# Two own sums moved ahead of other work in a kernel's head, with a rounding, two scalings and one diagonal

## The chip, the cores and the metric

The kernel runs on one core of one Trainium2 chip. The metric is the device time of one execution in microseconds (us), the median over the runs. The engines are TensorE (PE), VectorE (DVE), ScalarE (ACT), GpSimd (POOL) and SyncE (SP, which here only issues DMAs). Each engine works through its own queue in program order.

## The reference

Two stages. The first is a linear attention with a decaying state, for 4 batches, 8 heads, 768 steps and head size 48:

```python
for t in range(S):
    kt, vt, rt = (k[:, :, t], v[:, :, t], r[:, :, t])
    cur = np.einsum('bhd,bhe->bhde', u[None] * kt, vt)
    y[:, :, t] = np.einsum('bhd,bhde->bhe', rt, state + cur)
    state = w[None, :, :, None] * state + np.einsum('bhd,bhe->bhde', kt, vt)
```

Its output, as 3072 tokens of 384 numbers, goes through a gated feed-forward block with 1536 hidden numbers:

```python
g = x @ w_gate
silu = g * (1.0 / (1.0 + np.exp(-g)))
val = x @ w_val
return silu * val @ w_out
```

The three weight matrices arrive as 64-bit floats and are rounded to 32 bits on the chip.

## The kernel before, in words

The attention is cut into 24 units. Unit `i` is 128 steps of one batch: `divmod(i, 4)` gives the piece of the sequence and the batch. For one unit the kernel does this:

- `load(i)`, `load_v(i)`: SP issues the DMAs of k, r and v.
- `own_begin(i)`, `own_end(i)` (together `own_product`, L254 and L257): POOL multiplies r by k, then by u. `own_sum(i)` (L265): DVE sums over the head size. The result `du` is each step's product with itself, one number for each head.
- `diagonal(i)` writes `du` on the diagonal of `At[i % 2]`, the 128x128 score matrices of 8 heads. Units below 4 have four heads done by ACT (L364, one activation for each head) and four by POOL (L371, one instruction).
- `turn(i)`: PE transposes k and r (L385); for units below 4 DVE multiplies the results by tables of powers of w (L387).
- `scores(i)`: PE multiplies keys and rows (L454); then DVE copies the part above the diagonal into `At`, under a mask, in two instructions (L464). These are called the masks of unit i below. They need the diagonal to be in place.
- `outputs(i)`: PE multiplies `At` by v (L507), and ACT copies the result to xT (L511).
- `update(i)`: PE multiplies scaled keys by v (L522); DVE, and for later pieces POOL, bring the states Z up to date (L532 to L535). `scale_k(i)` and `scale_r(i)` (L341, L344) scale k and r on POOL by tables in SBUF. The four `scale_k` of the head work in place in the tile `hats`.

The weights come in 18 chunks of 768 KB. For each, `load_weights` issues the DMA (L179), into one of three buffers. Rounding a chunk takes ACT (`round_high` for each half, L199, through one of two PSUM banks; `round_low`, L205), DVE (`round_dve` for each half, L214 and L215) and POOL (`add_low` for a half, L223, or `round_pool` for a whole chunk, L242). `round_act` is all of ACT's and DVE's part of one chunk, and the issue of a later chunk's DMA.

`gate_value(g, f)` is one group of the feed-forward block: 12 matmuls on PE (L545), a Silu on ACT (L551) and a product on DVE (L552). `queue` puts the groups into a list, and `feed` takes the next one whose weight chunks have been rounded.

The order of the first four units, called the head, is written out by hand from L1204 on: the instructions of each engine are queued in the order of these calls. From L1281 on a loop goes over the units, one `turn`, one `scores`, one `outputs` in each pass, with roundings and `feed` calls in the gaps. After the attention the rest of the feed-forward block follows.

These lines of the head are the ones in which the predicted steps lie, up to the loop:

```python
own_sum(0); own_begin(1); diagonal(0); own_end(1); flush()
...
scores(0); own_sum(1); diagonal(1); flush()
...
feed(1); own_sum(2); diagonal(2); flush(); own_product(3); turn(3)
scores(2); update(0); update(1); scale_k(4); own_sum(3)
feed(1); diagonal(3); flush(); scores(3); scale_k(2); outputs(2)
round_act(); scale_k(3); outputs(3); scale_r(4); round_act()
```

(`flush` queues the ACT activations of a diagonal. The calls stand one to a line in the code.)

Of the kernel before, what the change touches and what calls it, by code (L numbers as in the profile page):

```python
# [22 lines left out]
def fast(  # L23
# [28 lines left out]
    HP = H // 2  # L52
# [65 lines left out]
    def raw(i):  # L118

        if i < 4:  # L120
            return khat[i][:, :, 0:D], rhat[i % 2][:, :, 0:D]
        return k_ld[i % 2][:], r_ld[i % 2][:]
# [46 lines left out]
    def next_chunk(stage):  # L169
        n = done[stage]  # L170
        done[stage] = min(n + 1, NW)
        return n if n < NW else None

    def load_weights():
        n = next_chunk("load")
        if n is not None:
            src = chunks[n][0].bitcast(INT32)
            bits[n] = three.tile([P, WN, 2], INT32, name="w_bits", tag="w_bits")
            sp.dma_start(  # L179
                out=bits[n][:].rearrange("p (c f) two -> p c (f two)", c=src.shape[1]), in_=src  # L180
            )
# [13 lines left out]
    def round_high(n, half, bank):  # L195
        hi = halves(bits[n][:, :, 1], n)[half]
        mag = banks[2 + bank][:, 0 : WN // 2].bitcast(INT32)
        mags[n, half] = mag.rearrange("p (c f) -> p c f", c=hi.shape[1])
        act.activation(  # L199
            mags[n, half].bitcast(FP32), hi.bitcast(FP32), AF.Copy, scale=float(2.0**-112)  # L200
        )

    def round_low(n):
        lows[n] = two.tile([P, WN], INT32, name="w_low", tag="w_low")
        act.activation(  # L205
            lows[n][:], bits[n][:, :, 0].bitcast(UINT32), AF.Copy, scale=float(2.0**-29)
        )

    def round_dve(n, half):
        hi = mags.pop((n, half))  # L210
        f = hi.shape[2]
        dst = chunks[n][1].bitcast(INT32)
        dst = dst[:, :, half * f : half * f + f] if hi.shape[1] == 3 else dst[:, half : half + 1]
        dve.tensor_scalar(dst, hi, -(1 << 31), None, ALU.bitwise_and)  # L214
        dve.scalar_tensor_tensor(dst, hi, 3, dst, ALU.logical_shift_left, ALU.bitwise_or)  # L215
# [6 lines left out]
        low = lows[n][:].rearrange("p (c f) -> p c f", c=dst.shape[1])  # L222
        pool.tensor_tensor(dst[:, :, cols], dst[:, :, cols], low[:, :, cols], ALU.add)  # L223

    def round_act(next_load=1):
        n = next_chunk("act")
        if n is not None:
            round_high(n, 0, 0)
            round_low(n)
            round_dve(n, 0)  # L230
            round_high(n, 1, 1)
            round_dve(n, 1)
            del bits[n]
            for _ in range(next_load):
                load_weights()

    def round_pool():
        n = next_chunk("pool")
# [12 lines left out]
    def own_begin(i):  # L251
        kl, rl = raw(i)
        rks[i] = two.tile([P, H, D], FP32, name="rk", tag="rk")[:]
        pool.tensor_mul(rks[i], rl, kl)  # L254

    def own_end(i):
        pool.tensor_mul(rks[i], rks[i], ub)  # L257

    def own_product(i):
        own_begin(i)  # L260
        own_end(i)

    def own_sum(i):
        dus[i] = three.tile([P, H], FP32, name="du", tag="du")
        dve.tensor_reduce(dus[i][:], rks.pop(i), axis=AX.X, op=ALU.add)  # L265
# [71 lines left out]

        return HP - 1 - a if i >= BLOCKS and i % 2 == (i < SWAPPED) else a

    def scale_k(i):  # L340
        pool.tensor_mul(khat[i % 4][:, :, 0:D], raw(i)[0], kscale)  # L341

    def scale_r(i):
        pool.tensor_mul(rhat_of(i)[:, :, 0:D], raw(i)[1], rscale)  # L344
# [6 lines left out]
    def keep_natural_tables():  # L351
        for bank, dst in zip(banks, (kscale, rscale)):
            act.copy(dst, bank[:].rearrange("p (h x) -> p h x", h=H)[:, :, 0:D])
# [2 lines left out]
        scale_k(i)  # L356
        scale_r(i)

    def diagonal(i):

        du = dus.pop(i)
        on_act = HP if i < 4 else H
        small.extend(
            lambda h=h: act.activation(  # L364
                At[i % 2][:, h, :], ident[:], AF.Identity, scale=du[:, h : h + 1]
            )
            for h in range(on_act)
        )
        if on_act < H:
            n = H - on_act  # L370
            pool.tensor_mul(  # L371
                At[i % 2][:, on_act:H], ident[:].unsqueeze(1).to_broadcast([P, n, P]),
                du[:, on_act:H].unsqueeze(2).to_broadcast([P, n, P]),
            )
# [4 lines left out]
    def turn(i):  # L379
        kr = khat[i % 4], rhat_of(i)  # L380
        tps = [next_psum(HP, P) for _ in kr]
        turned[i] = three.tile([P, HP, P], FP32, name="rT", tag="rT")
        for tp, t, dst, table in zip(tps, kr, (kT[i % 2], turned[i]), (pw[:, :, 1 : P + 1], pv)):
            for a in range(HP):
                pe.transpose(tp[:, a, :], pair(t, a), ident[:])  # L385
            if i < 4:
                dve.tensor_mul(dst[:], tp[:], table)  # L387
            else:
                act.copy(dst[:], tp[:])
# [48 lines left out]
    def scores(i):  # L438

        while lazy:  # L440
            lazy.popleft()()
        ps = [next_psum(HP, P) for _ in range(2)]
        whole, left, right = slice(0, P), slice(0, 64), slice(64, P)
        if i < SWAPPED:
            parts = [(a, whole, whole) for a in range(HP)]
        else:
            parts = []
            for a in range(HP // 2):
                parts += [(a, left, whole), (a, right, right)]
                parts += [(a + HP // 2, right, whole), (a + HP // 2, left, left)]  # L450
        for a, keys, cols in parts:
            for e in range(2):
                rows = slice(64 * e, 64 * e + D)
                pe.matmul(  # L454
                    ps[e][keys, a, cols],
                    kT[i % 2][rows, at(i, a), keys], turned[i][rows, at(i, a), cols],
                    start=True, stop=True, skip_group_check=True,
                )

        def masked_copy(e):  # L460
            if i < SWAPPED:
                dst = At[i % 2][:].rearrange("p (a e) t -> p a e t", e=2)[:, :, e]
                m = mask[:, 0].bitcast(INT32).unsqueeze(1).to_broadcast([P, HP, P])
                dve.copy_predicated(dst, m, ps[e][:])  # L464
                return
            dst = At[i % 2][:].rearrange("p (o a e) t -> p o a e t", o=2, e=2)[:, :, :, e]
            m = mask[:].bitcast(INT32).unsqueeze(2).to_broadcast([P, 2, HP // 2, P])
            dve.copy_predicated(dst, m, ps[e][:].rearrange("p (o a) t -> p o a t", o=2))

        for e in range(2):  # L470
            lazy.append(lambda e=e: masked_copy(e))
        lazy.popleft()()
        if i < BLOCKS:
            lazy.popleft()()
# [38 lines left out]
    def update(i):  # L513
        c, b = divmod(i, B)
        if c == NCH - 1:
            return
        kh, vl, z = khat[i % 4], v_ld[i % 4], Z[b]
        ps = next_psum(HP, D)
        for a in range(HP):
            for q in range(4):  # L520
                e, half = divmod(q, 2)
                pe.matmul(  # L522
                    ps[32 * q : 32 * q + 32, a, :], kh[:, 2 * a + e, 32 * half : 32 * half + 32],
                    vl[:, a, 64 * e : 64 * e + D],
                    start=True, stop=True, skip_group_check=True,
                )
        for e in range(2):
            rows = slice(64 * e, 64 * e + D)
            ze = z[rows, :, D * e : D * e + D]
            w = w128[rows].unsqueeze(2).to_broadcast([D, HP, D])  # L530
            if c == 0:
                dve.tensor_mul(ze, ps[rows], w)  # L532
            else:
                dve.tensor_add(ze, ps[rows], ze)  # L534
                pool.tensor_mul(ze, ze, w)  # L535
# [663 lines left out]
    def flush():  # L1199
        while small:  # L1200
            small.popleft()()
# [4 lines left out]
    dve.tensor_copy(w128[:].unsqueeze(2), pw[:, :, 0:1])  # L1206
    own_sum(0)
    own_begin(1)
    diagonal(0)
    own_end(1)  # L1210
    flush()
    load(2)
    turn(1)
    keep_natural_tables()
    round_high(0, 0, 0)
    round_low(0)
    load(3)
# [1 line left out]
    load_v(2)  # L1219
    load_v(3)  # L1220
    scores(0)
    own_sum(1)
    diagonal(1)
    flush()
    round_dve(0, 0)
    add_low(0, 0)
    scores(1)
    outputs(0)
    round_high(1, 0, 1)
    round_low(1)  # L1230
    round_dve(1, 0)
    add_low(1, 0)
    own_product(2)
    outputs(1)
    turn(2)
    scale_k(0)
    scale_k(1)
    queue(0)
    for n in range(2):
        round_high(n, 1, n)  # L1240
# [6 lines left out]
    load(5)  # L1247
    feed(1)
    own_sum(2)
    diagonal(2)  # L1250
    flush()
    own_product(3)
    turn(3)
    scores(2)
    update(0)
    update(1)
    scale_k(4)
    own_sum(3)
    feed(1)
    diagonal(3)  # L1260
    flush()
    scores(3)
    scale_k(2)
    outputs(2)
    round_act()
    scale_k(3)
    outputs(3)
    scale_r(4)
    round_act()
    own_product(4)  # L1270
    round_pool()
    update(2)
    update(3)
    load_v(4)
    feed(1)
    round_pool()
# [503 lines left out]
```

## Time and profile before

| | |
|---|---|
| median of 4 runs | 592.11 us (591.30 to 592.57) |
| the profiled execution's own time | 592.64 us |
| its span, first to last instruction | 590.9 us |
| granted TensorE clock | 0.998 |
| busy: PE, DVE, ACT, POOL | 579.6, 421.8, 225.5, 355.2 us |
| HBM read, written | 28.31 MB, 4.72 MB |

The profile is that of one execution. A row of its timeline reads: start in us, duration in us, engine, line, operation, output tile and input tiles, shapes, count, and in brackets the idle time of the engine before it with what ended it. Several equal instructions in a row are one row. A row of the waits reads: who waited, for what, us in total, times, the longest. A row of the table by stage gives the stretch, its length, and for PE, PE's weight loads, DVE, ACT and POOL the busy us and the instructions, then the granted clock, the DMA engines' busy share and GB/s. The time between the start of one instruction and that of the next on an engine is often a little shorter than the duration, since they overlap.

### The profile page before, as it was taken

What the parts mean: (1) busy time and instruction counts of PE and PEld (TensorE: products, weight loads), DVE (VectorE), ACT (ScalarE), POOL (GpSimd) and SP (SyncE); (2) the same over time, 40 slices, a digit from 0 to 9 for tenths busy, and PEclk for the clock granted to TensorE, in tenths of its full rate; (3) what the DMA queues carried; (4) which work ended last, traced back from release to release, by engine and by line L of the source; (5) the groups of instructions that cost most, each with busy time, mean ns of one, the idle gap of its engine ahead of it and who ended that gap; (6) DMA issues with size and microseconds to landing.
All of it is one profiled execution on the core that took longest, in us unless ns stands there. A gap on an engine that the chain in (4) does not pass through costs nothing.

```text
span 590.9 us, 13188 instructions
## 1 busy us (share of the span) xinstructions
PE 579.6 (98%) x5210; PEld 520.6 (88%) x5210; DVE 421.8 (71%) x703; ACT 225.5 (38%) x517; POOL 355.2 (60%) x378
## 2 busy tenths in 40 slices
PE   8889999999999999999999999999999999999996
PEld 7778888899888899988899988889988899888896
DVE  6887786489588777577887477779257878377672
ACT  3479786221343422245332345423134320233410
POOL 5899888989999403877601996412678960011610
PEclk9999999999999999999999999999999999999999
DMA  8999979442342323133234233300100000100001
GB/s 199 225 230 248 282 237 90 67 67 50 75 78 33 56 44 73 47 62 55 40 54 92 58 60 49 48 11 2 54 2 0 2 1 1 55 0 1 1 1 57
DMA packets 148292, 41.48 MB, mean 70 GB/s; under 512 B 138497, under 2 KB 142082, under 8 KB 148226
## 3 DMA queue, kind: packets, MB, share of 16 engines
q1 hardware_dynamic: 144914, 36.27, 30.0%
q10 hardware_dynamic: 3312, 4.33, 2.0%
q8 instruction: 42, 0.69, 0.5%
q14 instruction: 24, 0.20, 0.1%
HBM read 28.31 MB, written 4.72 MB: 56 GB/s over the span
## 4 chain that ended last, share of the span: by engine, by line
PE 91%; POOL 3%; DVE 2%; SPq 2%; issue 1%; DMA 0%; ACT 0%; POOLq 0%; DVEq 0%
PE bank L801 28%; PE bank L620 18%; PE ring L801 13%; PE bank L545 10%; PE bank L1027 9%; PE ring L507 6%; PE ring L454 3%; SPq L411 2%; PE ring L385 1%; POOL s L731 1%; PE ring L522 1%; PE ring L296 1%; POOL At L371 1%; DVE At L464 1%; DVE hv L825 0%
## 5 line engine op out<-in xcount | busy, mean ns | idle before, releaser
L825 DVE TENSOR_TENSOR hv<-hv,bank 128x512 f32<-128x512 f32 x132 | 87.2, 681 | 26.2 <-PE bank L801 15.2
L545 PE MATMUL bank<-xT,wgv 128*128 128x256 f32 x288 | 66.2, 384 | 0.0
L364 ACT ACTIVATE At<-ident,du 128x128 f32<-128x128 f32 x176 | 59.9, 398 | 16.6 <-DVE du L265 7.9
L801 PE MATMUL bank<-xf,wgv 128*128 128x256 f32 x256 | 65.9, 382 | 0.0
L825 ACT COPY hv<-bank 128x512 f32<-128x512 f32 x72 | 40.1, 585 | 57.5 <-PE bank L801 51.2
L545 PEld LDWEIGHTS bank<-xT,wgv 128*128 128x128 f32 x288 | 53.4, 190 | 7.9
L731 POOL TENSOR_TENSOR s<-wgv 128x256 f32<-128x256 f32 x39 | 29.8, 787 | 49.0 <-PE bank L620 48.9
L801 PEld LDWEIGHTS bank<-xf,wgv 128*128 128x128 f32 x256 | 47.8, 190 | 7.0 <-DVE kT L1072 0.6
L1081 POOL TENSOR_TENSOR hv<-At,hats 128x512 f32<-128x512 f32 x8 | 10.2, 1273 | 66.3 <-ACT At L1080 66.3
L535 POOL TENSOR_TENSOR Z<-Z,w 48x192 f32<-48x192 f32 x32 | 16.9, 528 | 36.8 <-DVE Z L534 35.6
L507 PE MATMUL ring<-At,v_ld 128*32 128x128 f32 x768 | 35.6, 273 | 3.4 <-DVE At L464 3.2
L832 ACT ACTIVATE hv<-hv 128x512 f32<-128x512 f32 (+1 forms) x33 | 21.2, 668 | 45.3 <-DVE hv L825 45.2
L801 PE MATMUL bank<-xT,wgv 128*128 128x256 f32 x144 | 35.8, 381 | 0.0
L801 PE MATMUL bank<-xT,s 128*128 128x256 f32 x152 | 35.5, 381 | 0.2 <-POOL s L731 0.2
L507 PEld LDWEIGHTS ring<-At,v_ld 128*32 128x32 f32 x768 | 30.5, 110 | 5.0 <-DVE At L464 4.9
L620 PE MATMUL bank<-wt,hs 128*128 128x192 f32 x192 | 33.7, 328 | 0.6 <-DVE hs L594 0.6
L620 PE MATMUL bank<-wo,hs 128*128 128x192 f32 x192 | 33.9, 327 | 0.0
L620 PE MATMUL bank<-wo,hv 128*128 128x192 f32 x192 | 33.4, 327 | 0.0
L801 PEld LDWEIGHTS bank<-xT,s 128*128 128x128 f32 x152 | 28.6, 190 | 5.1 <-issue 0.7
L620 PEld LDWEIGHTS bank<-wt,hs 128*128 128x128 f32 x192 | 31.3, 190 | 1.4 <-ACT At L364 0.8
L620 PEld LDWEIGHTS bank<-wo,hv 128*128 128x128 f32 x192 | 31.6, 190 | 0.4
L620 PEld LDWEIGHTS bank<-wo,hs 128*128 128x128 f32 x192 | 31.6, 190 | 0.3
(224 smaller groups left out, 1397.4 us busy)
## 6 DMA issues: line engine op xcount, KB each, us to landing
hats<-hats SPq DMA_DIRECT2D x192, 32.0 KB, 2.0
w_bits<-in_moe_w_gate_dram SPq DMA_DIRECT2D x6, 768.0 KB, 5.8
w_bits<-in_moe_w_val_dram SPq DMA_DIRECT2D x6, 768.0 KB, 7.3
w_bits<-in_moe_w_out_dram SPq DMA_DIRECT2D x6, 768.0 KB, 6.8
out_dram<-hv ACTq DMA_DIRECT2D x21, 192.0 KB, 1.9
v_ld<-in_v_dram SPq DMA_DIRECT2D x24, 96.0 KB, 5.8
k_ld<-in_k_dram SPq DMA_DIRECT2D x8, 192.0 KB, 3.6
r_ld<-in_r_dram SPq DMA_DIRECT2D x8, 192.0 KB, 4.7
```

The source lines that it names most:

```text
L364: lambda h=h: act.activation(At[i % 2][:, h, :], ident[:], AF.Identity, scale=du[:, h : h + 1])
L411: sp.dma_start(out=bass.AP(tensor=dst.tensor, offset=dst.offset, ap=[list(dst.ap[0]), [-P, 2 * HP], [1, 32]],), in_=bass.AP(tensor=src.ten ...
L454: pe.matmul(ps[e][keys, a, cols], kT[i % 2][rows, at(i, a), keys], turned[i][rows, at(i, a), cols], start=True, stop=True, skip_group_chec ...
L507: pe.matmul(ps[32 * q : 32 * q + 32, cc, :], *x, start=start, stop=stop, skip_group_check=True,)
L535: pool.tensor_mul(ze, ze, w)
L545: pe.matmul(gv[:, o, :].rearrange("p (i t) -> p i t", i=2), wt[:, c, P * f : P * (f + 1)], xT[:, 2 * g % NX : 2 * g % NX + 2, c, :], start ...
L620: pe.matmul(ps, lhs[:, f, :], rhs[:, f, :], start=(f == 0 and n in (0, 1, 4)), stop=(f == FH - 1), skip_group_check=True,)
L731: op(made[o], made[a], made[b])
L801: pe.matmul(ps[:, o], u[:, o], v, start=first and o == 0, stop=True, skip_group_check=True,)
L825: do(out, *(pair_of(wide[a][:]) if isinstance(a, str) else a for a in args))
L832: todo.append((at, lambda: act.activation(gate, gate, AF.Silu)))
L1027: pe.matmul(ps, (h[what][q] if h[what] is D_ else h[what][:, q])[:, f, :], wide["o"][what][:, f, :], start=first and f == 0 and (split or ...
```

## The change

All of it is in the head. `round_act` is split into `round_first` (first half of a chunk, and its low words) and `round_second` (second half, and the issue of a later load); `scale_k` takes the engine, and `diagonal` the number of heads on ACT.

- The second own product of unit 1 goes ahead of diagonal 0, own sum 1 ahead of the first rounding and of unit 0's scores. The copies of the tables from PSUM go behind diagonal 1 and behind the first `round_high` of chunk 1. Unit 1's scores and masks go ahead of the first `round_dve`.
- `scale_k(0)` and `scale_k(1)` run on DVE, after `turn(3)`, instead of on POOL after `turn(2)`.
- Diagonal 2 is done by ACT for all 8 heads.
- Own sum 3 goes ahead of unit 2's scores and masks; the gate-value group after them goes ahead of the two updates.
- The first half of chunk 2 is rounded ahead of unit 3's scores, the second half behind them; chunk 3 is rounded behind `outputs(3)`. `scale_k(4)`, and `own_product(4)`, go later, and POOL's rounding of chunk 2 goes ahead of `own_product(4)`.

```diff
+    def round_first(n):
+        round_high(n, 0, 0)
+        round_low(n)
+        round_dve(n, 0)
+
+    def round_second(n):
+        round_high(n, 1, 1)
+        round_dve(n, 1)
+        del bits[n]
+        load_weights()
...
-    def scale_k(i):
-        pool.tensor_mul(khat[i % 4][:, :, 0:D], raw(i)[0], kscale)
+    def scale_k(i, on=pool):
+        on.tensor_mul(khat[i % 4][:, :, 0:D], raw(i)[0], kscale)
...
-    def diagonal(i):
+    def diagonal(i, on_act=None):
...
-        on_act = HP if i < 4 else H
+        on_act = on_act or (HP if i < 4 else H)
...
     own_begin(1)
+    own_end(1)
     diagonal(0)
-    own_end(1)
     flush()
     load(2)
     turn(1)
-    keep_natural_tables()
+    own_sum(1)
     round_high(0, 0, 0)
     round_low(0)
...
     scores(0)
-    own_sum(1)
     diagonal(1)
     flush()
+    round_high(1, 0, 1)
+    keep_natural_tables()
+    scores(1)
     round_dve(0, 0)
     add_low(0, 0)
-    scores(1)
     outputs(0)
-    round_high(1, 0, 1)
     round_low(1)
...
     turn(2)
-    scale_k(0)
-    scale_k(1)
     queue(0)
...
     own_sum(2)
-    diagonal(2)
+    diagonal(2, H)
     flush()
     own_product(3)
     turn(3)
+    scale_k(0, dve)
+    scale_k(1, dve)
+    own_sum(3)
     scores(2)
+    feed(1)
     update(0)
     update(1)
-    scale_k(4)
-    own_sum(3)
-    feed(1)
     diagonal(3)
     flush()
+    ahead = next_chunk("act")
+    round_first(ahead)
     scores(3)
+    round_second(ahead)
+    outputs(2)
     scale_k(2)
-    outputs(2)
-    round_act()
     scale_k(3)
     outputs(3)
+    scale_k(4)
     scale_r(4)
+    round_pool()
     round_act()
-    own_product(4)
-    round_pool()
     update(2)
     update(3)
+    own_product(4)
     load_v(4)
     feed(1)
     round_pool()
```

More of the change, by code (lines that the diff above doesn't have):

```diff
@@ L223, in add_low, with round_act @@
         pool.tensor_tensor(dst[:, :, cols], dst[:, :, cols], low[:, :, cols], ALU.add)
-    def round_act(next_load=1):
+    def round_first(n):
[7 more added lines that the diff above has]
+        load_weights()
+    def round_act():
         n = next_chunk("act")
         if n is not None:
[L228 to L235, printed above, removed]
+            round_first(n)
+            round_second(n)
     def round_pool():
```

## The prediction

> **What bounds the kernel now.** I read the page first, then the busy table by stage, then what TensorE waits for, then the timeline of the head.
>
> ```profile
> PE 579.6 (98%) x5210; PEld 520.6 (88%) x5210; DVE 421.8 (71%) x703; ACT 225.5 (38%) x517; POOL 355.2 (60%) x378
> ```
>
> TensorE (PE) is busy for 579.6 of 590.9 us, so only its idle time is to be had. The table by stage says where that lies:
>
> ```profile
> 14.00:18.40 4.40, 2.85 (x64) 1.84 (x65) 4.21 (x8) 2.90 (x7) 2.04 (x2) 1.00 1.00 188
> 18.40:28.00 9.60, 9.44 (x122) 8.01 (x120) 6.93 (x13) 3.02 (x8) 9.33 (x10) 1.00 1.01 247
> 28.00:34.00 6.00, 4.25 (x145) 3.54 (x144) 5.09 (x12) 4.25 (x11) 5.59 (x7) 1.00 0.89 194
> 34.00:100.00 66.00, 66.00 (x709) 57.17 (x701) 52.12 (x107) 52.42 (x124) 58.83 (x51) 1.00 0.87 224
> ```
>
> The first pair of numbers is the stretch and its length, the next is PE's busy time. PE idles 1.55 + 0.16 + 1.75 us between 14 and 34 us, and not at all from 34 to 100. So the head sets when a full PE stream begins, and each us taken off before 34.03 comes off the end, as long as that stream stays fed. What PE waits for in the head:
>
> ```profile
> PE ring L507 <- DVE At L464: 3.2, 4, 1.5
> ```
>
> That is `outputs` waiting for the masks (L464), twice: for unit 1 and for unit 3. The timeline shows what the masks waited for:
>
> ```profile
> 16.00 1.35 DVE L464 COPY_PREDICATED At<-mask,ring 128x512 f32<-128x512 int32 x2
> 16.79 0.41 PE L507 MATMUL ring<-At,v_ld 128*32 128x128 f32 x4 [1.25 <-DVE At L464]
> 18.52 1.01 POOL L223 TENSOR_TENSOR wgv<-wgv,w_low 128x384 int32<-128x384 int32 x1 [1.47 <-DVE wgv L215]
> 26.47 1.35 DVE L464 COPY_PREDICATED At<-mask,ring 128x512 f32<-128x512 int32 x2 [1.86 <-POOL At L371]
> 29.21 0.56 DVE L265 TENSOR_REDUCE du<-rk 128x8 f32<-128x384 f32 x1
> 29.85 1.04 POOL L371 TENSOR_TENSOR At<-ident,du 128x512 f32<-128x512 f32 x1 [0.41 <-DVE du L265]
> 30.94 1.36 DVE L464 COPY_PREDICATED At<-mask,ring 128x512 f32<-128x512 int32 x2 [0.72 <-POOL At L371]
> 31.73 0.41 PE L507 MATMUL ring<-At,v_ld 128*32 128x128 f32 x4 [1.53 <-DVE At L464]
> ```
>
> Unit 3's masks start at 30.94 because own sum, POOL diagonal and masks follow one another, and the own sum came only at 29.21, behind unit 2's masks (26.47, held by POOL) and four Z products.
>
> **Step 1, units 0 and 1.** POOL does unit 1's second own product (1.00) before its half of diagonal 0, which then ends 0.5 us later, at 11.62; unit 0's masks start at 13.08 on PE's scores, so nothing is lost. Own sum 1 moves into VectorE's (DVE) 0.49 us gap before 13.08: rT product 11.89 + 0.60, own sum 12.49 to 13.03. POOL's diagonal 1 follows 0.07 later, 13.10 to 14.14 (1.04). Unit 1's masks then start when DVE is through with unit 0's (1.23 from start to next), at 14.31 instead of 16.00. The table copies on ScalarE (ACT, 0.83) go behind; their room is ACT's 1.57 us idle before 14.88, and the first roundings find their weights landed (issues at 5.02 and 6.03, 6.2 and 7.3 us to landing).
>
> **Step 2, first roundings.** DVE: masks 14.31 + 1.24 = 15.55; a half rounding takes 0.59 + 0.47 to the next, so chunk 0 starts at 15.55 and chunk 1 at 16.61, ending 16.61 + 0.59 + 0.56 = 17.76. POOL's add for chunk 1 comes 0.15 later: 17.91 instead of 18.52. On PE `outputs(1)` follows its mask at 15.7, `turn(2)` runs at 16.7 (its second load is issued at 13.20, lands 3.9 later, at 17.1), and the first gate-value group starts at 17.9 instead of 19.33, held by POOL's add of chunk 0 (16.61 - 0.47 + 0.56 + 0.14 + 1.00 = 17.84).
>
> **Step 3, POOL's queue.** Two `scale_k` (1.99) and diagonal 2 (1.04) leave it. From 17.91, with start-to-start steps of 0.96, 1.09, 0.95, 0.97 and 0.97 from the same rows: own product 2 at 18.87 and 19.96, the adds at 20.91 and 21.88, own product 3 at 22.85 and 23.94, ending 24.94 (before: 28.48). Diagonal 2 costs ACT four more activations of 0.295 each; it starts at 22.0 and its seventh is done 2.2 later, well ahead of its masks; ACT's 3.34 us idle before 28.13 hides it.
>
> **Step 4, DVE up to own sum 3.** From 17.67: two products of `turn(2)` (1.20), two half roundings (2.12), the gate-value product held by its Silu to 21.14, own sum 2 at 21.48, products of `turn(3)` at 21.94 (1.20), so `scale_k(0)` is issued at 23.14. Alone, a 128x384 product between two SBUF tiles should take 0.55 (128x256: 0.42 at 226 us, 128x512: 0.69 at 202.57, both beside an idle POOL); two end at 24.24, and DVE would wait for own product 3 until 24.97 anyway: cost nothing. But they run beside POOL, and the trace shows such a meeting:
>
> ```profile
> 196.97 1.01 POOL L254 TENSOR_TENSOR rk<-r_ld,k_ld 128x384 f32<-128x384 f32 x1
> 197.04 1.48 DVE L825 TENSOR_TENSOR hv<-hv 128x512 f32<-128x512 f32 x1 [0.78 <-ACT hv L832]
> 198.05 1.33 POOL L257 TENSOR_TENSOR rk<-rk,scales 128x384 f32<-128x384 f32 x1
> ```
>
> DVE's product takes 1.48 instead of 0.69, ending 0.54 after POOL's first; POOL's second takes 1.33 instead of 1.00, ending 0.86 after DVE's (6.15 to 8.56 shows the same). They take turns. With 0.40 for 384 elements: own product 3 first half ends 23.85, `scale_k(0)` 24.25, second half 25.11, `scale_k(1)` 25.51, and own sum 3 starts at 25.44, 0.47 late. The bounds are 0 (no meeting) and about 1.9 (both POOL halves at the longest such row, 1.71 at 127.77, so 2 x 0.71, and the second product 0.4 to 0.5 behind them); I take 0.47, from the nearest row.
>
> [...]
>
> **Step 5, to unit 3's masks.** Own sum 3 at 25.44; unit 2's masks now stand behind it, 25.90 (before 26.47); gate-value product 27.14; four Z products 27.48 (1.50); the first half rounding of chunk 2, now ahead of unit 3's masks, 28.98 (1.06); masks at 30.04 instead of 30.94. Diagonal 3 (POOL 26.1 to 27.1) is no longer what they wait for: DVE's own queue is late next. The rounding's input is ready: ACT makes it at 27.2 after its part of diagonal 3, its chunk lands at 22.9 (issue 15.66 + 7.2). Putting the second gate-value group before the two updates costs nothing on PE: DVE's Z products are later than PE either way, and `scores(3)`, which must wait for unit 2's masks (27.25), precedes masks that start only at 30.04.
>
> **The sum.** `outputs(3)` starts 0.90 earlier, at 30.83. The rest to the full stream is the same matmuls, so the stream starts at 33.13 instead of 34.03; xT of unit 3, now ahead of chunk 3's rounding on ACT, is ready at 32.95. POOL must keep up: `scale_r(4)` ends at 31.0, `round_pool` of chunk 2 waits for DVE's second half until 32.5, own product 4 behind it ends at 36.4 (before 35.85, its reader comes at 40.34), chunk 3 is done at 38.2 (before 39.42); PE asks for it at 39.3. SP's issues keep their order; the fetch that waited for ACT until 33.22 comes near 29.7. So span 590.9 - 0.9 = 590.0, execution 592.64 - 0.9 = 591.7; against the median of the runs, 592.11, which lies 0.5 below the profiled one: 591.2.
>
> **Rivals.** *The engines do not meet*: own sum 3 starts at 24.97, the gain is 1.37, the time 590.7. For: the two streams could fall between one another; against: every such pair at 6, 122 and 197 us met. *The saving is given back* in the weight stream: 592.1. Against: no PE wait from 34 to 100 us; for: DMA is 0.87 busy there and its landings up to 30 us do not move. *Slower: POOL's queue stands at `round_pool` of chunk 2*, put ahead of own product 4. For: its input comes from a rounding that now stands behind unit 3's masks on DVE, and nothing behind it can pass. Started at 33.7 it makes PE wait at 39.3, at 34.6 the gain is gone; started no earlier than now (35.82) chunk 3 is done at 41.5, PE waits 2.2, and the time is 593.4. Against: DVE arrives 1.2 us before the first of these points.
>
> **How the numbers follow.** About 0.2% (1.18 us) is what a measurement of this kernel can tell from no change. Chances: forecast 0.60, no meeting 0.18, given back 0.10, POOL standing 0.12. The forecast is 0.9 us ahead, 0.28 short of that line, and the runs before spread over 1.3 us: 0.27 of its 0.60 falls beyond the line. No meeting gives 0.17 more: faster 0.44. Same is 0.33 + 0.01 + 0.10 = 0.44; slower 0.12. The range starts at 590.1 (no meeting, less half of that spread) and reaches 592.5: given back, and the 1.9 bound of step 4 (592.11 - 1.37 + 1.9 = 592.6).
>
> **What would show it.** Right: unit 1's masks near 14.3, POOL's add of chunk 1 near 17.9, own product 3 ending near 25, both L341 rows on DVE at 0.8 to 1.1, unit 3's masks near 30.0, PE without gaps from 33.1. Wrong: masks 3 after 30.9, a PE wait between 34 and 60 us, or both L341 rows at 0.55 beside undisturbed POOL rows.

## The result, and the profile after

The changed kernel takes 591.41 us (median of 44 runs, 590.32 to 593.11); the kernel before took 592.35 (66 runs, 591.13 to 594.44). The ratio is 0.9984, with a 95% interval of 0.9979 to 0.9989, which is 0.94 us less. The profiled execution took 591.35 us and its span is 589.6 (before: 592.64 and 590.9).

The page's busy line first, as before:

```profile
PE 579.3 (98%) x5210; PEld 520.7 (88%) x5210; DVE 423.9 (72%) x705; ACT 226.9 (38%) x521; POOL 352.6 (60%) x375
```

PE's work is the same. POOL lost three instructions, DVE gained two and ACT four: two scalings and half a diagonal moved. The table by stage says where PE's idle time went (stretch and its length, then busy us of PE, PE's weight loads, DVE, ACT, POOL, the granted clock, DMA share, GB/s):

```profile
14.00:18.40 4.40, 3.92 (x74) 2.93 (x72) 4.33 (x9) 4.23 (x10) 1.63 (x3) 1.00 0.98 194
18.40:28.00 9.60, 9.12 (x126) 7.58 (x125) 9.37 (x17) 5.11 (x16) 8.42 (x9) 1.00 1.12 259
28.00:34.00 6.00, 4.43 (x140) 3.69 (x137) 4.74 (x10) 2.95 (x6) 4.52 (x5) 1.00 1.07 308
34.00:100.00 66.00, 66.00 (x703) 57.18 (x702) 51.89 (x107) 52.24 (x125) 58.37 (x52) 1.00 0.85 211
```

Between 14 and 18.4 us PE now idles 0.48 instead of 1.55, from 18.4 to 28 it idles 0.48 instead of 0.16, from 28 to 34 it idles 1.57 instead of 1.75, and from 34 to 100 still nothing. 0.36 of the second 0.48 is new: `scores(3)` waits for unit 2's masks. DVE is busy for 9.37 of the 9.60 us in the second stretch (before: 6.93): it now carries the head. What PE waits for up to 45 us:

```profile
PE ring L512 <- ACT xT L516: 1.4, 1, 1.4
PE ring L512 <- DVE At L469: 0.4, 2, 0.2
PE ring L459 <- DVE At L469: 0.4, 1, 0.4
```

(The lines are shifted by the change: `outputs` is L512, `scores` L459, the masks are L469, own sum L270, scalings L346.) The 3.2 us that `outputs` waited for masks have become 0.4, but the 1.4 put down to xT belongs to unit 3's masks too: ACT's last copy to xT before it ended at 30.03, 0.85 us before PE started, and PE starts 0.83 after the masks do, as it did before (0.79). In masks3_first below, where the masks come 1.06 sooner, this wait shrinks by 1.10. DVE's timeline of the head:

```profile
13.05 2.63 DVE L469 COPY_PREDICATED At<-mask,ring 128x512 f32<-128x512 int32 x4
15.56 0.56 DVE L214 TENSOR_SCALAR wgv<-bank 128x384 int32<-128x384 int32 x1
...
16.63 0.55 DVE L214 TENSOR_SCALAR wgv<-bank 128x384 int32<-128x384 int32 x1
...
23.22 2.32 DVE L346 TENSOR_TENSOR hats<-hats,scales 128x384 f32<-128x384 f32 x2
25.47 0.54 DVE L270 TENSOR_REDUCE du<-rk 128x8 f32<-128x384 f32 x1
25.93 1.33 DVE L469 COPY_PREDICATED At<-mask,ring 128x512 f32<-128x512 int32 x2
...
28.99 0.56 DVE L214 TENSOR_SCALAR wgv<-bank 128x384 int32<-128x384 int32 x1
...
30.05 1.32 DVE L469 COPY_PREDICATED At<-mask,ring 128x512 f32<-128x512 int32 x2
```

Units 0 and 1 are masked in one go, the roundings follow, the two scalings take 2.32 us instead of 1.1, and unit 3's masks start at 30.05 (before: 30.94). POOL and PE beside it:

```profile
16.86 2.06 POOL L223 TENSOR_TENSOR wgv<-wgv,w_low 128x384 int32<-128x384 int32 x2 [2.72 <-DVE wgv L215]
...
22.85 1.01 POOL L259 TENSOR_TENSOR rk<-hats 128x384 f32<-128x384 f32 x1
23.93 1.20 POOL L262 TENSOR_TENSOR rk<-rk,scales 128x384 f32<-128x384 f32 x1
...
32.55 1.83 POOL L247 TENSOR_TENSOR wgv<-wgv,w_low 128x768 int32<-128x768 int32 x1 [1.48 <-DVE wgv L215]
```

```profile
30.88 0.41 PE L512 MATMUL ring<-At,v_ld 128*32 128x128 f32 x4 [1.39 <-ACT xT L516]
...
33.16 3.07 PE L550 MATMUL bank<-xT,wgv 128*128 128x256 f32 x13
```

POOL's add for chunk 1 starts at 17.91 (the second of the pair; before 18.52), own product 3 ends at 25.13 (before 28.48), and PE's unbroken stream starts at 33.16 instead of 34.03. That is 0.87 of the 1.3 us between the two spans. Of the rest, 0.34 is two short PE waits of the profile before (0.22 at 370.8 us, 0.12 at 516.8) that this one does not have; 0.09 is not accounted for.

### The profile page after: what moved, and what is told of

Its sections match the earlier page's. It is cut to its first block, busy times and chain, and to the rows that moved or that the text cites. A ratio compares the mean times of both kernels' runs of the same rounds, so it can differ in the third digit from the quotient of the medians.

```text
span 589.6 us, 13192 instructions
## 1 busy us (share of the span) xinstructions
PE 579.3 (98%) x5210; PEld 520.7 (88%) x5210; DVE 423.9 (72%) x705; ACT 226.9 (38%) x521; POOL 352.6 (60%) x375
## 4 chain that ended last, share of the span: by engine, by line
PE 93%; SPq 2%; DVE 2%; DMA 1%; issue 1%; ACT 0%; DVEq 0%
PE bank L806 32%; PE bank L625 18%; PE ring L806 13%; PE bank L550 10%; PE bank L1032 9%; PE ring L512 6%; PE ring L459 3%; SPq L141 1%; PE ring L527 1%; PE ring L390 1%; DMA v_ld<-in_v_dram 1%; SPq L148 1%; SPq L179 0%; DVE hv L830 0%; DVE hats L346 0%
## 5 line engine op out<-in xcount | busy, mean ns | idle before, releaser
L512 PE MATMUL ring<-At,v_ld 128*32 128x128 f32 x768 | 35.2, 273 | 2.0 <-ACT xT L516 1.4
L512 PEld LDWEIGHTS ring<-At,v_ld 128*32 128x32 f32 x768 | 30.4, 110 | 3.3 <-ACT xT L516 1.6
```

What stands on the lines that cost most here:

```text
L512: pe.matmul(ps[32 * q : 32 * q + 32, cc, :], *x, start=start, stop=stop, skip_group_check=True,)
```

## The experiments

The main theory: the gain is the predicted chain, 0.61 us from units 0 and 1 (the add for chunk 1 at 17.91), and the rest from the stretch between that add and unit 3's masks, in which two scalings of POOL are traded for a meeting of 0.47 on DVE. The rivals: the moved scalings cost or bring nothing, the diagonal is the larger part, or the gain is scatter of executions.

Two distances within one trace are compared, since both leave out most of what happens earlier: from the start of POOL's add for chunk 1 to the start of unit 3's masks, and to the start of the stream. A late landing or a fall of the clock still enters them, as changed_again and undo_diagonal2 show, and each rests on one profile. "Clock" is when the trace first shows PE at the full clock. All times are us; each experiment has 5 to 12 runs, and the ratio is to the kernel before, run beside it. The ratio is not the quotient of the two medians, and the two can differ (own_sum3_late: 1.0039, the medians 595.20 and 592.29 give 1.0049).

| kernel | clock | add | to masks 3 | to stream | median | ratio (95%) |
|---|---|---|---|---|---|---|
| before | 11.72 | 18.52 | 12.42 | 15.51 | 592.35 | 1 |
| changed | 11.67 | 17.91 | 12.14 | 15.25 | 591.41 | 0.9984 (0.9979 to 0.9989) |
| undo_units01 | 9.31 | 17.86 | 12.20 | 15.30 | 591.75 | 0.9988 (0.9978 to 0.9997) |
| undo_scale_pool | 8.85 | 17.05 | 13.58 | 16.69 | 593.00 | 1.0011 (1.0002 to 1.0020) |
| undo_diagonal2 | 8.36 | 17.91 | 13.88 | 16.99 | 592.86 | 1.0006 (0.9995 to 1.0018) |
| masks3_first | 10.25 | 17.42 | 11.08 | 14.17 | 589.83 | 0.9957 (0.9943 to 0.9971) |
| changed_again | 11.14 | 17.62 | 13.51 | 16.62 | 591.15 | 0.9979 (0.9968 to 0.9990) |
| own_sum3_late | 10.37 | 17.35 | 14.06 | 18.63 | 595.20 | 1.0039 (1.0026 to 1.0052) |
| scalings_in_gaps | 10.46 | 17.54 | 11.67 | 14.78 | 590.79 | 0.9973 (0.9963 to 0.9983) |
| head_reordered | 10.31 | 17.91 | 9.10 | 13.84 | 590.12 | 0.9975 (0.9959 to 0.9992) |
| masks3_first_and_gaps | 11.12 | 17.64 | 10.60 | 13.69 | 590.32 | 0.9961 (0.9947 to 0.9975) |
| reordered_group_first | 10.65 | 17.60 | 9.64 | see there | 590.33 | 0.9966 (0.9954 to 0.9978) |

**undo_units01**: the changed kernel with units 0 and 1 in their old order.

```diff
-    own_end(1)
     diagonal(0)
+    own_end(1)
...
-    own_sum(1)
+    keep_natural_tables()
     round_high(0, 0, 0)
...
     scores(0)
+    own_sum(1)
     diagonal(1)
     flush()
-    round_high(1, 0, 1)
-    keep_natural_tables()
-    scores(1)
     round_dve(0, 0)
     add_low(0, 0)
+    scores(1)
     outputs(0)
+    round_high(1, 0, 1)
```

> The first part alone is undone: units 0 and 1 in the order of before (diagonal 0 ahead of the second own product of unit 1, own sum 1 and unit 1's masks behind the first roundings), all later edits kept. The theory of the forecast (one chain of POOL and VectorE from the first rounding to unit 3's masks): POOL's add of chunk 1 goes back from 17.9 to 18.5 us, and own product 3, own sum 3, masks 3 (now at 30.05) and the full PE stream follow by 0.6, so 0.6 us slower than the changed kernel (592.0). Rival 1, the first part brings the whole gain, since PE runs 1.4 us earlier from there: 0.9 slower, 592.35 as before. Rival 2, only the later part counts because DVE and POOL wait there anyway: no difference.

Its distances are the changed kernel's (12.20 and 15.30), so nothing behind the add depends on this part. Its add came at 17.86, but with the full clock from 9.31. The changed order of units 0 and 1 with nearly that clock is in undo_scale_pool (8.85), and there the add came at 17.05, as the second of this pair:

```profile
15.99 2.07 POOL L223 TENSOR_TENSOR wgv<-wgv,w_low 128x384 int32<-128x384 int32 x2 [3.06 <-DVE wgv L215]
```

That is 0.81 apart, against 0.61 between the two kernels at 11.7, though 0.46 us of clock lies between those two profiles; 0.35 of the 0.81 is DVE waiting for ACT's `round_high` of chunk 1, which in the old order stands behind the copy of `outputs(0)`. Three more profiles of the changed order (masks3_first, changed_again, own_sum3_late) have the add at 17.35 to 17.62, earlier than 17.86 although their clock came 0.94 to 1.83 later; in undo_diagonal2 it came at 17.91, behind a stand of PE and a fall of its clock. By time the undoing costs 0.0004 of 592 us, 0.2 us, instead of the 0.6 expected, and the interval holds both that 0.6 and the changed kernel's ratio: the traces show the part's worth, the times don't separate it from nothing.

**undo_scale_pool**: the two scalings back on POOL.

```diff
     turn(2)
+    scale_k(0)
+    scale_k(1)
...
     turn(3)
-    scale_k(0, dve)
-    scale_k(1, dve)
     own_sum(3)
```

> scale_k(0) and scale_k(1) go back to POOL, ahead of its second adds; all else as in the changed kernel. The theory: POOL's queue sets own sum 3. It gets 1.95 us more, own product 3 ends near 26.9 instead of 25.1, own sum 3 starts at 26.9 instead of 25.47 (the meeting of DVE and POOL, 0.5, goes away), masks 3 near 31.5: 1.45 us slower than the changed kernel and 0.5 slower than before (592.9). Rival 1, POOL's load is hidden and the gain comes from the order alone: no difference. Rival 2, the meeting costs nothing on the path (own sum 3 would be late by the whole 1.95): 593.4.

DVE's timeline:

```profile
26.05 0.55 DVE L270 TENSOR_REDUCE du<-rk 128x8 f32<-128x384 f32 x1 [3.47 <-POOL rk L262]
...
30.63 1.33 DVE L469 COPY_PREDICATED At<-mask,ring 128x512 f32<-128x512 int32 x2
```

Own sum 3 comes 9.00 behind the add (changed: 7.56), masks 3 1.44 later, and the kernel takes 593.0, as the theory had it. It is slower than the kernel before: with own sum 3 ahead of unit 2's masks, DVE stands 3.47 us for POOL with everything else behind it. From add to stream it takes 16.69, 1.18 more than before, of which the earlier add gives 0.6 back: +0.6, and +0.65 is measured (0.0011 of 592). So own sum 3, in this order, needs the scalings off POOL. That the whole 1.18 is POOL's doing is not shown: this kernel also has the rounding ahead of unit 3's masks, which alone costs 1.06 (masks3_first).

**undo_diagonal2**: half of diagonal 2 back on POOL.

```diff
-    diagonal(2, H)
+    diagonal(2)
```

> Diagonal 2 is half on POOL again, as before; all else as in the changed kernel. The theory: POOL has one instruction of 1.04 more ahead of own product 3, DVE's scalings then meet that and own product 3, own sum 3 starts at about 26.4 instead of 25.47, masks 3 near 31.0: about 1.0 us slower than the changed kernel, 592.4, so that nearly all of the gain hangs on this edit too. Rival, the meeting takes up the added instruction, since DVE's scalings run while POOL does the diagonal: at most 0.4 slower.

```profile
21.46 2.07 POOL L223 TENSOR_TENSOR wgv<-wgv,w_low 128x384 int32<-128x384 int32 x2 [0.50 <-DVE wgv L215]
23.51 1.04 POOL L376 TENSOR_TENSOR At<-ident,du 128x512 f32<-128x512 f32 x1
24.50 1.38 POOL L259 TENSOR_TENSOR rk<-hats 128x384 f32<-128x384 f32 x1
25.96 1.20 POOL L262 TENSOR_TENSOR rk<-rk,scales 128x384 f32<-128x384 f32 x1
```

From the same add at 17.91, own product 3 ends 2.03 later than in the changed kernel (27.16): 1.0 for the diagonal, 0.64 for the second pair of adds, which waited for DVE, and 0.38 for the meeting, which now hits its first half as well (1.38 instead of 1.01). Masks 3 come 1.74 later: in the changed kernel own sum 3 started 0.34 after POOL's end, behind DVE's scalings, and now these are done before POOL is. The 0.64 comes from ahead of the moved diagonal: PE stood 2.11 us from 12.42 on, for a landing of v, its clock fell to half, and `turn(2)` and what DVE makes of it came late. The table by stage shows the clock in the column behind POOL's:

```profile
15.20:18.60 3.40, 3.40 (x58) 3.02 (x50) 2.38 (x5) 2.04 (x5) 1.70 (x2) 0.50 1.11 204
```

By time the undoing costs 1.3 us (0.0022 of 592), somewhat over the expected one; by the trace it is 1.10 (1.74 less 0.64). So POOL's queue decides here, and the diagonal is worth its length in it.

**masks3_first**: DVE's part of the rounding behind unit 3's masks, as it was before the change; ACT's part stays ahead.

```diff
-    round_first(ahead)
+    round_high(ahead, 0, 0)
+    round_low(ahead)
     scores(3)
+    round_dve(ahead, 0)
     round_second(ahead)
```

> One step on from the changed kernel: DVE's first half rounding of chunk 2 stands behind unit 3's masks, not ahead. The theory: from own sum 3 on it is DVE's own queue that masks 3 wait for; without the rounding's 1.06 us ahead they start at 29.0 instead of 30.05, PE's wait before the outputs of unit 3 falls from 1.39 to about 0.3, and the end comes 1.06 earlier, 590.35. POOL's rounding of chunk 2 comes no later, since DVE has both halves done at the same time. Rival 1, diagonal 3 on POOL or unit 3's scores on PE hold the masks: gain under 0.3. Rival 2, the saving is given back because PE asks for chunk 3 at 38.2, just when POOL has it: a PE wait near 38 us and a gain between 0.3 and 0.8.

```profile
27.00 1.47 DVE L537 TENSOR_TENSOR Z<-ring,w 48x192 f32<-48x192 f32 x4
28.50 1.35 DVE L469 COPY_PREDICATED At<-mask,ring 128x512 f32<-128x512 int32 x2
29.76 0.53 DVE L214 TENSOR_SCALAR wgv<-bank 128x384 int32<-128x384 int32 x1
```

```profile
29.30 0.41 PE L512 MATMUL ring<-At,v_ld 128*32 128x128 f32 x4 [0.29 <-DVE At L469]
```

The distances shrink by 1.06 and 1.08, the price of that rounding, and PE waits 0.29 instead of 1.39 before `outputs(3)`. The time falls 1.6 below the changed kernel's (0.0027 of 592), 0.5 more than expected. In the profile the add came 0.49 earlier too, with the full clock 1.4 us sooner; whether all five runs share that is not shown. **This version has the lowest median of all**, and its ratio's interval does not overlap the changed kernel's (it does overlap changed_again's, and later versions below are not apart from it). The step of the change that puts the rounding ahead of the masks costs 1.06, by the distances.

**changed_again**: the changed kernel, for a second profile.

> The changed kernel itself, beside the others of this call. The theory: 0.9 us faster than before again, and unit 3's masks 12.14 us behind POOL's add of chunk 1, as in its first profile (17.91 to 30.05), wherever the clock grant puts that add. Rival: the 0.9 was a matter of the clock's phase in one profile; then the distance between the two changes from profile to profile.

The time is the same again; the distance is not, 13.51 instead of the expected 12.14. The chief wait of PE in the head, and two rows of the timeline:

```profile
PE ring L390 <- DMA hats<-in_r_dram: 2.0, 1, 2.0
```

```profile
19.08 0.66 PE L390 MATMUL ring<-ident,hats 128*128 128x128 f32 x4 [1.97 <-DMA hats<-in_r_dram]
...
31.13 1.33 DVE L469 COPY_PREDICATED At<-mask,ring 128x512 f32<-128x512 int32 x2
```

The r of unit 2 landed at 19.04 (issued at 13.61; in the profile after it landed at 16.03), so `turn(2)` stood with half its transposes done. Before the change `turn(2)` ran at 18.40; now PE is there by 16.7, so a landing after that is no longer hidden. The distance moved with this landing, not with the clock's start (11.14), and the median kept its gain, so the rival is not borne out. This execution took 592.24, against the median of 591.15, and its stream started at 34.24, later than the 34.03 of the profile before the change.

**own_sum3_late**: own sum 3 back behind the Z products, all else as changed.

```diff
-    own_sum(3)
     scores(2)
     feed(1)
     update(0)
     update(1)
+    own_sum(3)
     diagonal(3)
```

> Own sum 3 goes back behind unit 2's masks and the updates, as before the change; all else as in the changed kernel. The theory: DVE's queue, not own sum 3, is what unit 3's masks wait for. DVE does the same instructions in another order, own sum 3 at 28.5, POOL's diagonal 3 at 29.1 to 30.2, and the masks at 30.2 instead of 30.05: only 0.1 to 0.2 slower than the changed kernel, 591.55. Rival, moving own sum 3 is what brings the gain: back to before, 0.9 slower.

A clear miss, of the theory and the rival: +3.3 us on the changed kernel (0.0055 of 592; the medians of the two on this chip are 4.05 apart). DVE's timeline, then ACT's and PE's:

```profile
27.99 0.55 DVE L270 TENSOR_REDUCE du<-rk 128x8 f32<-128x384 f32 x1
30.35 0.56 DVE L214 TENSOR_SCALAR wgv<-bank 128x384 int32<-128x384 int32 x1 [1.80 <-ACT bank L199]
...
31.41 1.33 DVE L469 COPY_PREDICATED At<-mask,ring 128x512 f32<-128x512 int32 x2
```

```profile
28.64 1.28 ACT L369 ACTIVATE At<-ident,du 128x128 f32<-128x128 f32 x4 [3.25 <-DVE du L270]
29.82 0.49 ACT L199 ACTIVATE bank<-w_bits 128x384 f32<-128x384 f32 x1
```

```profile
32.23 2.32 PE L512 MATMUL ring<-At,v_ld 128*32 128x128 f32 x30 [3.74 <-ACT xT L516]
```

The expectation left out ACT's queue. Own sum 3 releases ACT's half of diagonal 3, behind which stands `round_high` of chunk 2, for which DVE's rounding waits, behind which stand the masks: they came 1.92 later. PE stood 3.74 us for them, and 2.34 us into that stand, at 30.84, its clock fell:

```profile
30.90:37.60 6.70, 5.37 (x100) 4.61 (x101) 4.50 (x10) 3.19 (x7) 6.28 (x6) 0.50 0.70 212
```

The way from masks 3 to the stream took 4.57 instead of 3.11 with the same matmuls, so 1.46 of the 3.38 lost up to the stream (18.63 - 15.25) is that clock. So with the rounding ahead of the masks, own sum 3 has to be early.

**scalings_in_gaps**: the two scalings on POOL, but in its idle time before the add, with each table copied when needed.

```diff
     own_sum(1)
+    keep_natural_tables(0)
+    scale_k(0)
     round_high(0, 0, 0)
...
     round_high(1, 0, 1)
-    keep_natural_tables()
+    keep_natural_tables(1)
+    scale_k(1)
...
-    scale_k(0, dve)
-    scale_k(1, dve)
     own_sum(3)
```

> scale_k(0) and scale_k(1) on POOL, in its idle time ahead of and behind diagonal 1 (11.75 to 13.1 and 14.1 to 16.9 us), with the copy of kscale moved ahead of the first rounding on ACT; all else as in the changed kernel. So DVE and POOL do not meet, and neither has more to do on the path. The theory: own sum 3 starts on POOL's end, 24.97 instead of 25.47, and masks 3 and the end come 0.5 earlier: 590.9. Rival 1, the meeting cost nothing on the path: no difference. Rival 2, the copies on ACT hold up diagonal 1, and unit 1's masks with it: 0.3 to 0.5 slower.

```profile
11.77 1.02 POOL L346 TENSOR_TENSOR hats<-hats,scales 128x384 f32<-128x384 f32 x1 [0.16 <-ACT scales L357]
...
13.74 1.03 POOL L346 TENSOR_TENSOR hats<-hats,scales 128x384 f32<-128x384 f32 x1
...
22.47 1.02 POOL L259 TENSOR_TENSOR rk<-hats 128x384 f32<-128x384 f32 x1
23.57 1.00 POOL L262 TENSOR_TENSOR rk<-rk,scales 128x384 f32<-128x384 f32 x1
```

Own product 3 runs undisturbed, own sum 3 comes 7.06 behind the add instead of 7.56, and masks 3 0.47 sooner. The meeting therefore costs 0.50 at own sum 3; the prediction had 0.47. By time it is 590.79 against changed_again's 591.15 on the same chip, with overlapping intervals.

**head_reordered**: scalings in the gaps, and unit 3's masks directly behind unit 2's, the updates and the rounding later.

```diff
     feed(1)
-    update(0)
-    update(1)
     diagonal(3)
     flush()
+    scores(3)
+    outputs(2)
+    update(0)
+    update(1)
     ahead = next_chunk("act")
     round_first(ahead)
-    scores(3)
+    outputs(3)
     round_second(ahead)
-    outputs(2)
...
-    outputs(3)
...
     update(3)
-    own_product(4)
     load_v(4)
...
     feed(1)
+    own_product(4)
     own_sum(4)
```

> Built on scalings_in_gaps: diagonal 3, unit 3's scores and masks directly behind unit 2's, then the outputs of unit 2, the updates, and only then the rounding of chunk 2; own product 4 behind the rounding of chunk 3. The theory: nothing of DVE's queue stands ahead of masks 3 but what they need. They start at 27.0 instead of 30.05, PE has no wait over 0.5 us from 18 us on, and its full stream starts near 30.6 instead of 33.16: 2.5 us faster than the changed kernel, 588.9. Rival 1, the weights become the bound: PE asks for chunk 3 at 36.8 and POOL has it only near 37.4 or later, 0.6 to 1.5 given back. Rival 2, PE's scores or the rings of PSUM hold the masks: 590 or above.

Masks 3 start at 27.01, as meant (the first row below, DVE's), but PE's timeline has a new stand:

```profile
27.01 1.39 DVE L468 COPY_PREDICATED At<-mask,ring 128x512 f32<-128x512 int32 x2
```

```profile
29.39 0.32 PE L526 MATMUL ring<-v_ld,hats 128*32 128x48 f32 x6
31.01 0.80 PE L526 MATMUL ring<-v_ld,hats 128*32 128x48 f32 x56 [1.30 <-issue]
```

After eight matmuls of `update(2)` PE stands 1.30 us for nothing that the profile names. The median is 590.12 instead of the expected 588.9, some 1.2 more; the ratio's interval is wide because one of 12 runs took 595.86.

**masks3_first_and_gaps**: the edits of both.

> Both improvements together: the rounding of chunk 2 behind unit 3's masks on DVE (masks3_first) and the two scalings in POOL's idle time (scalings_in_gaps). The theory: the two lie one behind the other on DVE's queue, so they add up: unit 3's masks 10.6 us behind POOL's add of chunk 1 (12.14 in the changed kernel, 11.08 with the first alone), PE's stream 1.55 earlier than in the changed kernel, 589.7. Rival: with masks that early PE itself, which comes to the outputs of unit 3 about 11.5 us behind that add, is the bound, and the second edit brings under 0.2.

```profile
28.24 1.36 DVE L468 COPY_PREDICATED At<-mask,ring 128x512 f32<-128x512 int32 x2
```

```profile
31.33 2.86 PE L549 MATMUL bank<-xT,wgv 128*128 128x256 f32 x12
```

Both shortenings add up in the trace: 13.69 to the stream, 1.56 less than changed. The time does not show it: 0.9961 against 0.9957 for masks3_first alone, on different chips, is no difference. In the profiles, too, the stream starts 0.26 earlier than in masks3_first (31.59) and the span is 0.2 longer (588.3 and 588.1); what takes it back behind the head is not shown.

**reordered_group_first**: head_reordered, with the next gate-value group ahead of updates 2 and 3, to learn what the stand of 1.30 was.

```diff
-    update(2)
-    update(3)
     load_v(4)
     feed(1)
+    update(2)
+    update(3)
```

> The kernel head_reordered with the next gate-value group ahead of the updates of units 2 and 3. In head_reordered PE stood 1.30 us within the first of these updates, with no semaphore behind it in the profile, and an instruction fetch of PE's had just run. Theory 1, PE ran out of fetched instructions: the stand falls on about the same instruction count whatever comes there, so the group starts near 31 us as the updates did, and the time stays at 590.1. Theory 2, the updates' operands held it (a ring of PSUM or scaled keys): the group starts at 30.2, as soon as xT of unit 3 is there, and the time falls by 1.0 to 1.3, to 589.

```profile
30.44 2.86 PE L549 MATMUL bank<-xT,wgv 128*128 128x256 f32 x12 [0.57 <-ACT xT L515]
```

The stand of 1.30 is gone; the group starts after 0.57, though PE had lost 0.65 at `turn(2)` to a late r. Its start is near the 30.2 of the theory of an operand. The second group starts at 34.05, no earlier than in masks3_first_and_gaps (34.03), and the ratio, 0.9966, is not apart from head_reordered's, as the theory of the instructions had it. Whether the 1.30 was a wait for an operand of the update or for PE's instructions (a packet of 16 KB, taken here for these, was moved from 28.33 to 29.52 in head_reordered and from 27.79 to 29.17 here, on a queue that the profile calls "instruction") stays open.

## Why the prediction was right

**Units 0 and 1, first roundings.** Masks 14.31 as predicted, the roundings at 15.56 and 16.63 (15.55, 16.61), the add at 17.91 (17.91).

**POOL's queue.** Own product 3 at 22.85 and 23.93 (22.85, 23.94). That this is what the later gain hangs on is shown: a scaling pair back in the queue costs 1.44, the diagonal about one.

**The meeting.** Scalings issued at 23.22 (23.14), ended 25.54 (25.51), own sum 3 at 25.47 (25.44), and scalings_in_gaps prices the meeting at 0.50 (0.47). Its shape was a little off: the scalings took 1.05 and 1.35, where 0.8 to 1.1 was named.

**To the masks and the stream.** Masks 2 25.93 (25.90), gate-value product 27.16 (27.14), rounding 28.99 (28.98), masks 3 30.05 (30.04), `outputs(3)` 30.88 (30.83), stream 33.16 (33.13).

**The sum.** 0.9 was forecast; the stream gained 0.87 and the median 0.94. The 0.2 us between 591.2 and 591.41 is in the base: 592.11 was the median of 4 runs, 592.35 is that of 66. At 0.16% the gain lies on the near side of the 0.2% line, as the forecast itself did, though its interval keeps it clear of zero. That single rows came out to 0.05 us is partly luck: the two profiles happened to share the clock's start (11.72 and 11.67), and r of unit 2 landed in time. The upper end of the range, 592.5, is 0.1 below the 592.6 that its own sum gives; nothing turned on it.

**The rivals.** No meeting: the rows met. Given back: PE has no idle time from 34 to 100 us. POOL standing at `round_pool`: it started at 32.55 (32.5), 1.15 us before the point named.

**What the steps did not say.** The change is 0.61 from units 0 and 1 and only 0.26 (15.51 - 15.25) from everything behind, because a good step (own sum 3 and POOL's queue) pays for one that costs 1.06 (the rounding ahead of the masks). The prediction counted that rounding in its chain, but did not name its removal as the better version. And step 2 let r of unit 2 land in time at 17.1; changed_again shows 19.04, and masks 3 at 31.13, beyond the 30.9 that was named as wrong. Two parts of the change were not undone by themselves: the gate-value group ahead of the two updates, and POOL's later `scale_k(4)` and own product 4 with `round_pool` ahead of it.

## What to carry to other kernels

Compare distances between two events of the same trace, not times from its start: here they gave the scalings, the meeting and the rounding to within 0.05 us of what had been worked out, where the runs spread over 3. First see whether the two traces differ in a landing or in the clock between the two events: in changed_again a late r made the distance 1.37 longer. When several steps move together, cost each alone with the others in place, in both directions: with the scalings back on POOL the changed kernel is slower than the one before, and the rounding ahead of the masks is a loss inside a gain. Follow what an early result releases on every engine's queue, two steps on: it was ACT's queue, and the fall of PE's clock behind it, that made a harmless-looking move cost 3.3 us.

## What the runs showed of the hardware

**PE's full clock started at a different time in each of the 12 profiles.** It is there first between 8.36 and 11.72 us into the span, 3.36 apart. The mean clock hides it (0.998 to 1.000 where no drop follows in the head), but the transposes of units 0 and 1 show it; the groups of L390 up to 13 us (duration in ns min/median/max, first and last start), of the changed kernel, then of undo_scale_pool:

```profile
L390 PE MATMUL ring<-ident,hats x16: 391/421/422, 6.5 to 11.4; 128*128 128x128 f32 x16
```

```profile
L390 PE MATMUL ring<-ident,hats x16: 272/347/421, 6.5 to 10.2; 128*128 128x128 f32 x16
```

All 16 ran slow in the one, the later ones fast in the other, and unit 0's masks started at 13.05 and at 11.72. By POOL's add 0.86 was left (17.91 and 17.05). The profiles before and after the change have nearly the same start, so they could be subtracted.

**Two stands of PE came with a half clock.** In undo_diagonal2 PE stood 2.11 us (12.42 to 14.53), and from 15.19 the clock was half for 3.41 us; in own_sum3_late it stood 3.74 us, and from 30.84, during the stand, the clock was half for 6.83; after 1.97 us in changed_again it stayed full. At the ends of the kernels it fell 2.94 us after the end of the last matmul in the profile before (585.63 to 588.57), and 4.51 after it in the one after (584.01 to 588.52). So the length of a stand alone does not say when the clock falls. In the two heads the times between its changes are near whole multiples of 3.41 us: 6.83 (8.36 to 15.19) and 3.41 in undo_diagonal2, 20.47 (10.37 to 30.84) and 6.83 in own_sum3_late. What sets the stands of 2.11 and 1.97 apart is not shown.

**Products of DVE and POOL that met took turns, with a small overlap.** A 128x384 product of two SBUF tiles on DVE, issued while POOL's was running, took 0.83 to 1.36 in these profiles (1.05 and 1.35 in the changed kernel), and POOL's behind it 1.19 to 1.38 instead of 1.00. Where DVE's started first (undo_diagonal2) or POOL was done (changed_again), DVE's took 0.55. In the changed kernel DVE's ended 0.41 after POOL's and POOL's 0.86 after DVE's, each less than it takes alone (0.55 and 1.00); by scalings_in_gaps, both together lost 0.50 us.

**Landings scattered.** The r of unit 2 landed between 15.92 (masks3_first) and 19.04 us (changed_again) in the 12 profiles; at 17.1 in the one before, at 16.03 in the one after.
